# Weight loads and splits placed among the first two batches' chunks of scores in an attention-then-experts kernel

## The chip, the cores and the metric

One core of a Trainium2 chip runs the whole program. The metric is the device time of one execution in microseconds (us); lower is better. The times of before are a median of three runs, and one further execution was profiled. On this core TensorE multiplies matrices, VectorE and ScalarE work elementwise, GpSimd (POOL) issues the indirect stores, and SyncE (SP) issues all other transfers, in order.

## The reference

Four batches of 5056 tokens go through an attention over the 256 channels; each resulting row goes to one of eight experts (the one of the largest logit).

```python
qn = q / (np.linalg.norm(q, axis=1, keepdims=True) + 1e-06)
kn = k / (np.linalg.norm(k, axis=1, keepdims=True) + 1e-06)
s = kn.transpose(0, 2, 1) @ qn / tau        # [B, 256, 256]
a = softmax(s)
x = (v @ a).reshape(B * N, 256)
logits = x @ w_gate                          # [B*N, 8]
e = argmax(logits); gate = softmax(logits)[e]
out = gate * (np.maximum(x @ w1[e], 0) @ w2[e])   # w1 256x1024, w2 1024x256
```

## The kernel before, in words

**Attention of a batch** (`attention`, L182 to L394) is a generator. It first goes through 20 *chunks* of 256 tokens: loads of q and k (L194, L195, 256 KB each), squares on ScalarE (L203) that VectorE adds up to the channel norms (two adds, L207 and L208), and the scores. In a *native* chunk these are four fp32 matmuls (L214, eight pieces in the trace); in a *split* chunk ScalarE and VectorE first write q and k as two parts (L177, L178), which eight faster matmuls use (L218, L219). Batch 0 is native throughout, batch 1 native in chunks 1 to 13. Then come the norms (L227 to L246) and the softmax (L248 to L302), and ten *groups* of 512 tokens: a load of v (L312), v @ a and the gate's logits (`px`, L326 for batch 0, L329 for others), copies and squares on ScalarE (L331, L333), rows as two fp16 parts (L343, L344), the expert and place of each token, and four indirect stores by POOL into the sorted array `xs` (L392).

**Weights** (`weights`, L93 to L162) is a generator over 16 matrices (w1 and w2 of each expert). Each is loaded as two halves of 512 KB (L118, L120) into the place in `W` that the next matrix's parts will fill, so no load waits for a buffer. TensorE forms its Gram matrix from 16 pieces (L134), VectorE takes the diagonal (L137) for the scale of the expert, and each half is later *split* into two fp16 parts: ScalarE writes the high part (L105), VectorE the low one (L106), each 1024 elements per partition.

**Experts** (`block`, L538 to L600) work on *blocks* of 256 sorted rows of one expert: 48 matmuls with w1 (L561), relu and split (L568, L569), 48 with w2 (L584). `table` (L447) makes the list of a stage's blocks from the counts so far; stage 0 is made from batch 0's first six groups (`CUT`).

**The order.** A scheduler emits each engine's queue, in order, close to the order of the code. The opening (L648 to L653) takes all 20 chunks of batch 0, then 14 steps of the weights, then per step one of batch 0 (softmax and half groups), two of the weights and one chunk of batch 1: ten chunks in all. The weight loads are put behind the last q and k load (`last_load`). Then come the first table, batch 0's last four groups, and the blocks. During the blocks the remaining attention runs as side work, in amounts set by planned costs (a chunk 1280 units, a group 2920): `START` (L669) counts what was done ahead, and the first ten blocks share out the rest of batch 1, (START + 59800) / 10 = 4700 units a block.

**Buffers that matter here.** q, k and v share the three `raw` tiles (batch 0's chunks also use `rows` and `xg`); the diagonal and ScalarE's junk squares share one tile, `junk`; the blocks' copies of weight pieces have five tiles, `wp` (L548).

Of the kernel before, what the change touches and what calls it, by code (L numbers as in the profile page):

```python
# [20 lines left out]
P = 128  # L21
# [40 lines left out]
def attention_then_experts(ctx, tc, q, k, vT, tau, w_gate, w1, w2, kc, out):  # L62
# [27 lines left out]
    last_load = [None]  # L90

    def weights():
# [8 lines left out]
        def split_one():  # L101
            nonlocal ready
            if ready:
                hi, lo, src, sw = ready.pop(0)
                act.activation(hi, src, AF.Copy, scale=sw)  # L105
                vec.scalar_tensor_tensor(out=lo, in0=src, scalar=sw, in1=hi, op0=ALU.mult, op1=ALU.subtract)  # L106

        for n in range(2 * E):
            e, w = divmod(n, 2)
            if n < 2 * E - 1:  # L110
                raw = place(n + 1).bitcast(F32)
            else:
                raw = work.tile([P, 2048], F32, tag="hl", name="wraw", bufs=2)
            raw = raw.rearrange("p (h x) -> p h x", h=2)
            for h in range(2):
                with tc.issue_after(last_load[0]):
                    if w == 0:
                        sync.dma_start(out=raw[:, h, :], in_=w1[e, h * P : (h + 1) * P, :])  # L118
                    else:
                        sync.dma_start(  # L120
                            out=raw[:, h, :].rearrange("p (f d) -> p f d", d=C),
                            in_=w2[e, h * 512 : (h + 1) * 512, :].rearrange("(f p) d -> p f d", p=P),
                        )
                split_one()
# [7 lines left out]
            for i in range(16):  # L132
                part = top[:, i * P : (i + 1) * P]
                pe.matmul(own, part, part, start=(i == 0), stop=(i == 15))  # L134
            diag = work.tile([P, P], F32, tag="junk", name="w_diag", bufs=1)
# [8 lines left out]
            for h in range(2):  # L144
                if w == 0:
                    d5 = place(n).rearrange("p (q d s f) -> p q d s f", q=4, d=2, s=2)
                    hi, lo = d5[:, :, h, 0, :], d5[:, :, h, 1, :]
                    src = raw[:, h, :].rearrange("p (q f) -> p q f", q=4)
                else:
                    d4 = place(n).rearrange("p (f s d) -> p f s d", f=8, s=2)  # L150
                    hi, lo = d4[:, 4 * h : 4 * h + 4, 0, :], d4[:, 4 * h : 4 * h + 4, 1, :]
                    src = raw[:, h, :].rearrange("p (f d) -> p f d", f=4)
                later.append((hi, lo, src, sw))
            if w == 1:
                ready, later = ready + later, []
# [25 lines left out]
    def attention(b, s_split, x_split, acc):  # L181
# [5 lines left out]
        ssq = one.tile([P, 512], F32, tag="a_l", name="ssq")  # L187
        nch = len(s_split)
        for ch in range(nch):

            tag, bufs = (("raw", RAW), ("rows", 3), ("xg", 2), ("raw", RAW), ("rows", 3))[ch % 5 if b == 0 else 0]
            raw = work.tile([P, 2, 512], F32, tag=tag, name="raw", bufs=bufs)
            sl = slice(2 * ch, 2 * ch + 2)
            sync.dma_start(out=raw[:, :, 0:C], in_=qv[b][:, sl, :])  # L194
            load = sync.dma_start(out=raw[:, :, C:512], in_=kv[b][:, sl, :])  # L195
            if b == 0:
                last_load[0] = load.ins
# [5 lines left out]
            act.activation(sq, raw, AF.Square)  # L203
            if ch == 0:
# [18 lines left out]


        tp = ps_t.tile([P, 512], F32, tag="tp", name="ntp")
        for i in range(4):
            pe.matmul(tp[:, i : i + 1], ssq[:, i * P : (i + 1) * P], ones[:, 0:1], start=True, stop=True)  # L227
# [20 lines left out]
        soft = work.tile([P, 8, C], F32, tag="hl", name="soft", bufs=2)  # L248
        for c in range(2):
            dg = soft[:, 0, c * P : (c + 1) * P]  # L250
# [9 lines left out]
        if any(s_split):  # L260
            sums = [soft[:, 1 + c, :] for c in range(2)]
# [476 lines left out]
```

## Time and profile before

| | us |
|---|---|
| median of 3 runs | 1236.44 (1236.13 to 1242.23) |
| profiled execution | 1234.98 |
| its span in the profile | 1233.1 |
| batch 0's scores end on TensorE | 41.9 |
| first x matmul | 61.7 |
| first matmul of a block | 159.4 |

The profile names each instruction by its line of the kernel, with its operands (out <- in), and says for an idle engine what released it. Busy times of an engine are unions of its instructions' spans, so waiting inside the queue is what is left. TensorE's granted clock is given per stretch, 1.00 being 2.4 GHz.

### The profile page before, as it was taken

To read this page: it belongs to the slowest core of one execution; us is meant where nothing else is said; L and a number is where in the kernel's file an instruction comes from. 1 tells how busy PE (TensorE), PEld (TensorE's weight loads), DVE (VectorE), ACT (ScalarE), POOL (GpSimd) and SP (SyncE) were. 2 spreads that over 40 slices of the span, in tenths; PEclk is the share of its full clock that TensorE was granted. 3 is DMA by queue.
4 is the path that set the end of the run, shared out by engine and by line. 5 is a ranking of instruction groups with operands and counts; after the bars stand their busy time and mean duration, and the time that the engine had idled before them with its cause. 6 is when DMAs were issued, how large, how long until landed. Compare 5 with 4: busy or idle time off the path is not lost.

```text
span 1233.1 us, 28379 instructions
## 1 busy us (share of the span) xinstructions
PE 1163.7 (94%) x10182; PEld 1027.0 (83%) x10182; DVE 921.1 (75%) x2586; ACT 648.0 (53%) x1378; POOL 356.8 (29%) x326
## 2 busy tenths in 40 slices
PE   8778789988899999999999999999999999999998
PEld 7666577878788888988888888889888888888887
DVE  6787888867798878777788878767676666666886
ACT  5477864666655545656655545666533333332332
POOL 0022451244431112544432111455331111111111
PEclk9879999999999999999999999999999999999999
DMA  9968685434354533344254453342232222211121
GB/s 308 379 226 270 177 199 141 117 104 129 104 149 125 137 95 96 112 128 114 79 143 125 126 111 87 108 113 82 71 106 53 53 53 53 49 48 42 39 49 33
DMA packets 190688, 145.93 MB, mean 118 GB/s; under 512 B 117580, under 2 KB 168145, under 8 KB 190544
## 3 DMA queue, kind: packets, MB, share of 16 engines
q1 hardware_dynamic: 175152, 102.48, 32.7%
q0 software_dynamic: 15392, 41.60, 9.6%
q8 instruction: 81, 1.33, 0.5%
q14 instruction: 63, 0.52, 0.1%
HBM read 80.03 MB, written 43.29 MB: 100 GB/s over the span
## 4 chain that ended last, share of the span: by engine, by line
PE 47%; issue 26%; DVE 6%; POOL 5%; ACT 1%; DMA 1%; POOLq 0%; another core or an unknown queue 0%; DVEq 0%; SPq 0%; ACTq 0%
PE hp L561 17%; PE y L584 17%; PE px L329 6%; POOL out L595 4%; PE sp L218 3%; PE sp L219 2%; DVE ht L569 1%; POOL xs L392 1%; DVE hl L178 1%; DVE rows L344 1%; DVE wp L549 1%; DMA xs<-rows,r_si 1%; ACT ht L568 0%; ACT rows L343 0%; DMA out<-o,mt 0%
## 5 line engine op out<-in xcount | busy, mean ns | idle before, releaser
L584 PE MATMUL y<-wp,ht 128*128 128x256 f16 x3888 | 450.5, 273 | 8.3 <-DVE ht L569 4.6
L561 PE MATMUL hp<-xT,wp 128*128 128x256 f16 (+1 forms) x4320 | 450.1, 262 | 5.8 <-issue 2.5
L584 PEld LDWEIGHTS <-ht 128*128 128x128 f16 x3888 | 373.2, 98 | 68.1 <-issue 11.1
L561 PEld LDWEIGHTS <-wp 128*128 128x128 f16 x4320 | 382.2, 98 | 53.9 <-issue 11.0
L549 DVE COPY wp<-W 128x1024 f16 x720 | 298.6, 428 | 104.1 <-PE y L584 68.5
L595 POOL DMA_INDIRECT out<-o,mt x162 | 182.2, 1125 | 664.0 <-ACT o L593 631.2
L568 ACT ACTIVATE ht<-hp 128x512 f16<-128x512 f32 x324 | 191.5, 595 | 197.2 <-PE hp L561 143.0
L569 DVE SCALAR_TENSOR_TENSOR ht<-hp,ht 128x512 f16<-128x512 f32 x324 | 221.7, 687 | 42.1 <-ACT ht L568 36.7
L392 POOL DMA_INDIRECT xs<-rows,r_si x160 | 174.4, 1090 | 207.9 <-DVE scales L83 82.4
L593 ACT ACTIVATE o<-y,b_fac 128x256 f32<-128x256 f32 x162 | 68.8, 469 | 176.6 <-PE y L584 164.2
L329 PE MATMUL px<-a_h,hl 128*128 128x264 f32 x480 | 100.4, 297 | 6.0 <-ACT xg L331 4.0
L343 ACT ACTIVATE rows<-xg,x_sc 128x256 f16<-128x256 f32 x160 | 69.1, 497 | 34.9 <-DVE x_sc L83 31.1
L329 PEld LDWEIGHTS px<-a_h,hl 128*128 128x128 f32 x480 | 79.7, 190 | 8.3 <-ACT xg L331 5.1
L177 ACT CAST hl<-raw 128x1024 fp32r<-128x1024 f32 x47 | 49.1, 1045 | 49.4 <-PE sp L219 40.1
L214 PE MATMUL sp<-raw 128*128 128x256 f32 x264 | 64.6, 403 | 10.8 <-DMA raw<-in_k 10.8
L178 DVE TENSOR_TENSOR hl<-raw,hl 128x1024 fp32r<-128x1024 f32 x47 | 57.4, 1222 | 22.9 <-ACT hl L177 22.9
L218 PE MATMUL sp<-hl 128*128 128x512 f32 x188 | 73.3, 422 | 0.0
L331 ACT COPY xg<-px 128x264 f32<-128x264 f32 x160 | 58.1, 367 | 26.2 <-PE px L329 7.0
L203 ACT ACTIVATE raw<-raw 128x1024 f32<-128x1024 f32 x47 | 49.7, 1058 | 41.2 <-DVE hl L178 39.4
L329 PE MATMUL px<-a_l,hl 128*128 128x264 f32 x240 | 68.9, 287 | 0.0
L344 DVE SCALAR_TENSOR_TENSOR rows<-xg,x_sc,rows 128x256 f16<-128x256 f32 x160 | 68.7, 477 | 0.2
L333 ACT ACTIVATE xjunk<-xg 128x256 bf16<-128x256 f32 x160 | 66.5, 416 | 3.0
(138 smaller groups left out, 942.9 us busy)
## 6 DMA issues: line engine op xcount, KB each, us to landing
raw<-in_q SPq DMA_DIRECT2D x80, 256.0 KB
raw<-in_k SPq DMA_DIRECT2D x80, 256.0 KB
vraw<-in_vT SPq DMA_DIRECT2D x40, 512.0 KB
W<-in_w SPq DMA_DIRECT2D x30, 512.0 KB
out<-o,mt POOLq DMA_INDIRECT x162
xs<-rows,r_si POOLq DMA_INDIRECT x160
xT<-xs SPq DMA_TRANSPOSE x90
xs<-pad SPq DMA_DIRECT2D x9, 129.0 KB
```

The costliest lines, as they stand in the source:

```text
L178: vec.tensor_tensor(out=hl[:, 1], in0=raw, in1=hl[:, 0], op=ALU.subtract)
L218: pe.matmul(sp[c], hl[:, 0, j, kc0 : kc0 + P], hl[:, :, j, 0:C], start=first, stop=False)
L329: pe.matmul(px, hl[:, vh, c, ts], ah[:, c, :], start=(n == 0), stop=(n == 5))
L343: act.activation(r16[:, t, 0:C], x, AF.Copy, scale=sc[:, t : t + 1])
L344: vec.scalar_tensor_tensor(out=r16[:, t, C : 2 * C], in0=x, scalar=sc[:, t : t + 1], in1=r16[:, t, 0:C], op0=ALU.mult, op1=ALU.subtract,)
L392: ins = pool.indirect_dma_start(out=xs[:, :], out_offset=bass.IndirectOffsetOnAxis(ap=si[:n, t : t + 1], axis=0), in_=rows[:n, t, :], in_o ...
L549: vec.tensor_copy(out=t, in_=Wf[:, ds(e * 8192 + n * 1024, 1024)])
L561: pe.matmul(hp[:, f % nf, :], wp[:, dc, wh, (f % 2) * P : (f % 2 + 1) * P], xT[:, 2 * xh + dc, :], start=(n == 0), stop=(n == 5),)
L568: act.activation(ht[:, 0], hp, AF.Relu)
L569: vec.scalar_tensor_tensor(out=ht[:, 1], in0=hp, scalar=0.0, in1=ht[:, 0], op0=ALU.max, op1=ALU.subtract)
L584: pe.matmul(ys[j], hts[f // nf][:, hh, f % nf, j * P : (j + 1) * P], wp[:, f % 2, wh, :], start=(f == 0 and n == 0), stop=(f == 7 and n == 2),
L595: pool.indirect_dma_start(out=out[:, :], out_offset=bass.IndirectOffsetOnAxis(ap=mt.bitcast(I32)[:, j, 1:2], axis=0), in_=o, in_offset=Non ...
```

## The change

- **Loads.** All of the opening's loads are issued in one written order (`load`). From chunk 2 of batch 0 on, one weight load follows each chunk's q and k; the rest follow two to a step among v and batch 1's chunks.
- **Steps.** Batch 0's chunks 2 to 19 each come with one step of the weights (nine matrices loaded by then, most of their Grams and some splits done). 15 further steps take two of the weights, batch 0's softmax and six groups, and 13 chunks of batch 1 (`OPENING`) instead of 10. `START` follows: 4316 units a block.
- **Splits** take a whole matrix, 2048 elements per partition, in one instruction each on ScalarE and VectorE; only the last matrix is split in four quarters, from `ht` tiles.
- **Buffers.** Batch 0's chunks use three `raw` and three `rows` tiles, its v (groups 0 to 5) the blocks' `wp` tiles with loads up to two groups ahead, its softmax the blocks' `xT` and `o` tiles, its sum of squares an `xg` tile. The diagonal has a tile of its own.
- **Norms of batch 0**: one add of 1024 elements per chunk instead of two of 512, and eight small matmuls instead of four at the end.

```diff
+    def load(out, in_):
+        if opening[0] is None:
+            ins = sync.dma_start(out=out, in_=in_)
+        else:
+            with tc.issue_after(opening[0]):
+                ins = sync.dma_start(out=out, in_=in_)
+        opening[0] = ins.ins
...
-            diag = work.tile([P, P], F32, tag="junk", name="w_diag", bufs=1)
+            diag = work.tile([P, P], F32, tag="diag", name="w_diag", bufs=1)
...
-                later.append((hi, lo, src, sw))
+            d4 = place(n).rearrange("p (k s x) -> p k s x", k=8, s=2)
+            if n < 2 * E - 1:
+                src = place(n + 1).bitcast(F32).rearrange("p (k x) -> p k x", k=8)
+                later.append((d4[:, :, 0, :], d4[:, :, 1, :], src, sw))
+            else:
+                for i in range(4):
+                    ks = slice(2 * i, 2 * i + 2)
+                    later.append((d4[:, ks, 0, :], d4[:, ks, 1, :], raw[i].rearrange("p (k x) -> p k x", k=2), sw))
...
-            tag, bufs = (("raw", RAW), ("rows", 3), ("xg", 2), ("raw", RAW), ("rows", 3))[ch % 5 if b == 0 else 0]
-            raw = work.tile([P, 2, 512], F32, tag=tag, name="raw", bufs=bufs)
+            tag = "rows" if b == 0 and ch % 2 else "raw"
+            raw = work.tile([P, 2, 512], F32, tag=tag, name="raw", bufs=3)
...
+            if b == 0:
+                if ch > 0:
+                    vec.tensor_tensor(out=ssq, in0=ssq, in1=sq, op=ALU.add)
...
+        def v_load(g):
+
+            if g < CUT:
+                raw = [work.tile([P, 512], F32, tag="wp", name="vraw", bufs=WP) for _ in range(2)]
+            else:
+                both = work.tile([P, 2, 512], F32, tag="raw", name="vraw", bufs=RAW)
+                raw = [both[:, 0, :], both[:, 1, :]]
...
+        if b == 0:
+            for g in range(2):
+                v_ahead[g] = v_load(g)
...
+            dgs = work.tile([P, C], F32, tag="o", name="dgs", bufs=2)
+            sums_t, s2, aT = [work.tile([P, 2, C], F32, tag="xT", name=nm, bufs=3) for nm in ("sums", "s2", "aT")]
...
+                raw = v_ahead.pop(g, None) or v_load(g)
+                if g + 2 < G and early():
+                    v_ahead[g + 2] = v_load(g + 2)
...
-    for step in range(2, nch + 1 + 2 * CUT):
+    for ch in range(1, nch):
         take(first, 1)
-        take(wts, 0 if step < nch else 14 if step == nch else 2)
-        if step > nch + 2:
-            take(second, 1)
+        take(wts, 1 if ch > 1 else 0)
+    take(first, 1)
+    for step in range(2 * CUT + 3):
+        if step > 2:
+            take(first, 1)
+        take(wts, 2)
+        take(second, 1 if step < OPENING else 0)
     run(wts)
...
-    START = -(2 * CUT - 2) * 2 * 640
+    START = -OPENING * 2 * 640
```

**How the queues change.** SP's queue where batch 0's loads end, before (`raw` is q and k of a chunk, `W` a half of a weight matrix):

```order
L194 DMA raw_301<-in_q 128x2x256
L195 DMA raw_301<-in_k 128x2x256
L194 DMA raw_312<-in_q 128x2x256
L195 DMA raw_312<-in_k 128x2x256
L118 DMA W_79<-in_w1 128x1024 x2
L120 DMA W_79<-in_w2 128x4x256 x2
L118 DMA W_79<-in_w1 128x1024 x2
L120 DMA W_79<-in_w2 128x4x256 x2
```

and in the changed kernel, some chunks earlier:

```order
L97 DMA raw_210<-in_q 128x2x256
L97 DMA raw_210<-in_k 128x2x256
L97 DMA W_79<-in_w1 128x4x256
L97 DMA raw_223<-in_q 128x2x256
L97 DMA raw_223<-in_k 128x2x256
L97 DMA W_79<-in_w1 128x4x256
L97 DMA raw_254<-in_q 128x2x256
L97 DMA raw_254<-in_k 128x2x256
L97 DMA W_79<-in_w2 128x4x256
```

The weights stood behind the last chunk; now one load of them follows each chunk's pair.

SP's queue where batch 0's v loads begin to wait for buffers, before:

```order
L118 DMA W_79<-in_w1 128x1024 x2
L312 DMA vraw_538<-in_vT 128x2x512
L120 DMA W_79<-in_w2 128x4x256 x2
L118 DMA W_79<-in_w1 128x1024 x2
L312 DMA vraw_665<-in_vT 128x2x512
L120 DMA W_79<-in_w2 128x4x256 x2
L194 DMA raw_722<-in_q 128x2x256
L195 DMA raw_722<-in_k 128x2x256
L118 DMA W_79<-in_w1 128x1024 x2
```

and now, at the load of v for group 2 (two tiles of 256 KB, `vraw_710` and `vraw_711`):

```order
L97 DMA raw_662<-in_q 128x2x256
L97 DMA raw_662<-in_k 128x2x256
L97 DMA W_79<-in_w2 128x4x256 x2
L97 DMA raw_699<-in_q 128x2x256
L97 DMA raw_699<-in_k 128x2x256
L97 DMA vraw_710<-in_vT 128x512
L97 DMA vraw_711<-in_vT 128x512
L97 DMA W_79<-in_w1 128x4x256 x2
L97 DMA raw_764<-in_q 128x2x256
```

Group 2's v stands ahead of the loads of the next weight matrix.

VectorE's queue around batch 0's first group of x, before (`W` with `scales` is a split, `w_diag` a diagonal, `x_sc`, `r_` the group's small steps):

```order
L137 SCALAR_TENSOR_TENSOR w_diag_653,w_dsum_567<-gram_566,kt_104 128x128
L389 TENSOR_REDUCE r_si_631<-r_sl_629 128x4
L82 TENSOR_SCALAR pw_m_656<-gram_566 128x2
L83 TENSOR_SCALAR scales_377<-pw_m_656 128x2
L106 SCALAR_TENSOR_TENSOR W_79<-W_79,scales_377 128x4x256 x2
L352 TENSOR_REDUCE r_m_751<-xg_667 128x4
L354 TENSOR_TENSOR r_d_753<-xg_667,r_m_751 128x32
L357 SCALAR_TENSOR_TENSOR r_eq_755<-r_d_753,kt_104 128x32
L359 TENSOR_REDUCE r_r_757<-r_eq_755 128x4
L106 SCALAR_TENSOR_TENSOR W_79<-W_79,scales_377 128x4x256
L137 SCALAR_TENSOR_TENSOR w_diag_711,w_dsum_694<-gram_693,kt_104 128x128
L106 SCALAR_TENSOR_TENSOR W_79<-W_79,scales_377 128x4x256
```

and now, from the end of the softmax on:

```order
L356 COPY aT_563<-atp_581 128x512
L242 TENSOR_TENSOR ssq_621<-ssq_621,sq_665 128x512
L364 COPY a_x_568<-gtp_587 128x2x8
L113 SCALAR_TENSOR_TENSOR W_79<-W_79,scales_133 128x8x256
L154 SCALAR_TENSOR_TENSOR w_diag_693,w_dsum_643<-gram_642,kt_92 128x128
L241 TENSOR_TENSOR ssq_621<-ssq_621,sq_702 128x512
L82 TENSOR_SCALAR pw_m_696<-gram_642 128x2
L242 TENSOR_TENSOR ssq_621<-ssq_621,sq_702 128x512
L83 TENSOR_SCALAR scales_133<-pw_m_696 128x2
L113 SCALAR_TENSOR_TENSOR W_79<-W_79,scales_133 128x8x256
```

The splits are half as many and twice as long, and chunks of batch 1 (`ssq`) now stand between them from the softmax on.

## Rows read from the trace of the kernel before

**Rows 1.** The page, part 1: busy us, share of the span, instructions.

```profile
PE 1163.7 (94%) x10182; PEld 1027.0 (83%) x10182; DVE 921.1 (75%) x2586; ACT 648.0 (53%) x1378; POOL 356.8 (29%) x326
```

**Rows 2.** Busy time by stage: stretch, its us, each engine, clock, DMA.

```profile
core 0: us, PE busy (x) PEld busy (x) DVE busy (x) ACT busy (x) POOL busy (x), PEclk, DMA share, GB/s
0.00:10.00 10.00, 5.36 (x13) 4.37 (x14) 2.73 (x9) 3.51 (x4) 0.20 (x4) 1.00 0.76 227
10.00:30.00 20.00, 20.00 (x94) 17.60 (x93) 16.84 (x25) 13.77 (x14) 0.00 (x0) 1.00 1.08 346
30.00:60.00 30.00, 23.81 (x180) 21.45 (x178) 22.20 (x60) 12.76 (x16) 0.00 (x0) 0.89 1.07 379
42.70:61.70 19.00, 11.60 (x119) 10.66 (x117) 15.79 (x50) 9.36 (x12) 0.00 (x0) 0.80 1.06 378
61.70:159.40 97.70, 78.31 (x433) 62.10 (x434) 79.53 (x289) 78.35 (x192) 35.47 (x30) 0.90 0.73 222
159.40:320.00 160.60, 145.50 (x1206) 127.89 (x1207) 123.88 (x418) 100.16 (x247) 60.00 (x57) 0.99 0.51 136
320.00:1233.00 913.00, 890.19 (x8261) 793.10 (x8258) 674.19 (x1785) 437.85 (x909) 261.13 (x236) 1.00 0.34 89
```

**Rows 3.** TensorE timeline: start us, us, line, operation, operands, count.

```profile
4.64 37.27 PE L214 MATMUL sp<-raw 128*128 128x256 f32 x160 [4.64 <-DMA raw<-in_k]
...
42.56 1.08 PE L134 MATMUL gram<-W 128*128 128x128 bf16 x16
...
61.66 6.80 PE L326 MATMUL px<-a_x,vraw 128*128 128x264 f32 x16
...
159.40 1.47 PE L561 MATMUL hp<-xT,wp 128*128 128x256 f16 x12
...
167.11 1.89 PE L214 MATMUL sp<-raw 128*128 128x256 f32 x8
```

**Rows 4.** Waits of TensorE, 61.7 to 159.4 us: total us, times, longest.

```profile
PE gram L134 <- DVE w_diag L137: 6.8, 2, 4.2
PE sp L214 <- DMA raw<-in_k: 6.2, 3, 2.3
```

**Rows 5.** Waits of SP (the queue of loads), 61.7 to 159.4 us.

```profile
SPq L194 <- PE sp L214: 11.1, 4, 6.3
SPq L312 <- PE px L326: 10.4, 2, 8.0
```

**Rows 6.** The page, part 6: loads, their count, KB of each.

```profile
raw<-in_k SPq DMA_DIRECT2D x80, 256.0 KB
...
W<-in_w SPq DMA_DIRECT2D x30, 512.0 KB
```

**Rows 7.** VectorE groups, 61.7 to 159.4 us: count, busy us, mean ns, idle before.

```profile
L106 DVE SCALAR_TENSOR_TENSOR W<-W,scales 128x1024 f16<-128x1024 f32 x24 | 30.1, 1281 | 6.2 <-ACT W L105 4.9 <-issue 1.3
L344 DVE SCALAR_TENSOR_TENSOR rows<-xg,x_sc,rows 128x256 f16<-128x256 f32 x32 | 13.7, 478 | 0.0
...
L207 DVE TENSOR_TENSOR ssq<-ssq,sq 128x512 f32<-128x512 f32 x9 | 6.2, 685 | 0.0
...
L137 DVE SCALAR_TENSOR_TENSOR w_diag<-gram,kt 128x128 f32<-128x128 f32 x10 | 2.8, 285 | 2.9 <-PE gram L134 2.9
```

**Rows 8.** Busy time and granted clock of three 10 us stretches (columns of rows 2).

```profile
50.00:60.00 10.00, 7.28 (x62) 6.77 (x61) 7.69 (x20) 5.11 (x9) 0.00 (x0) 0.66 1.06 383
...
80.00:90.00 10.00, 7.43 (x38) 6.39 (x38) 9.80 (x34) 7.53 (x13) 3.36 (x3) 0.66 0.84 280
90.00:100.00 10.00, 7.78 (x48) 6.41 (x47) 7.31 (x17) 8.45 (x19) 4.33 (x4) 1.00 0.93 309
```

**Rows 9.** ScalarE groups, 61.7 to 159.4 us.

```profile
L105 ACT ACTIVATE W<-W,scales 128x1024 f16<-128x1024 f32 x23 | 25.6, 1140 | 6.9 <-DVE scales L83 3.7 <-DVE W L106 3.2
...
L343 ACT ACTIVATE rows<-xg,x_sc 128x256 f16<-128x256 f32 x35 | 14.9, 496 | 2.8 <-DVE x_sc L83 2.6 <-DVE r_r L359 0.2
```

**Rows 10.** TensorE group of native chunks, 61.7 to 159.4 us.

```profile
L214 PE MATMUL sp<-raw 128*128 128x256 f32 x76 | 20.6, 421 | 6.2 <-DMA raw<-in_k 6.2
```

More of the change, by code (lines that the diff above doesn't have):

```diff
@@ L166, in attention_then_experts, with early @@
     WP = 5
+    blocks_begun = [False]
+    def early():
+        return not blocks_begun[0]
     EARLY = 2
+    OPENING = 13
     NATIVE = 14
@@ L186, in attention @@
         sp = [pool_.tile([P, 2, C], F32, tag=tag, name=f"sp{c}") for c, (pool_, tag) in enumerate(acc)]
-        ssq = one.tile([P, 512], F32, tag="a_l", name="ssq")
+        if b == 0:
+            ssq = work.tile([P, 2, 512], F32, tag="xg", name="ssq", bufs=2)
+        else:
+            ssq = one.tile([P, 512], F32, tag="a_l", name="ssq")
         nch = len(s_split)
         for ch in range(nch):
-            tag, bufs = (("raw", RAW), ("rows", 3), ("xg", 2), ("raw", RAW), ("rows", 3))[ch % 5 if b == 0 else 0]
-            raw = work.tile([P, 2, 512], F32, tag=tag, name="raw", bufs=bufs)
+            tag = "rows" if b == 0 and ch % 2 else "raw"
+            raw = work.tile([P, 2, 512], F32, tag=tag, name="raw", bufs=3)
             sl = slice(2 * ch, 2 * ch + 2)
[L194 to L197, printed above, removed]
+            for part, src in ((raw[:, :, 0:C], qv[b]), (raw[:, :, C:512], kv[b])):
+                if early():
+                    load(part, src[:, sl, :])
+                else:
+                    sync.dma_start(out=part, in_=src[:, sl, :])
             if s_split[ch]:
@@ L222, in attention @@
             yield 2 * 640
+        v_ahead = {}
+        def v_load(g):
+            if g < CUT:
+                raw = [work.tile([P, 512], F32, tag="wp", name="vraw", bufs=WP) for _ in range(2)]
+            else:
+                both = work.tile([P, 2, 512], F32, tag="raw", name="vraw", bufs=RAW)
+                raw = [both[:, 0, :], both[:, 1, :]]
+            for c in range(2):
+                if early():
+                    load(raw[c], vv[b][:, c, g * 512 : (g + 1) * 512])
+                else:
+                    sync.dma_start(out=raw[c], in_=vv[b][:, c, g * 512 : (g + 1) * 512])
+            return raw
+        if b == 0:
+            for g in range(2):
+                v_ahead[g] = v_load(g)
         tp = ps_t.tile([P, 512], F32, tag="tp", name="ntp")
         for i in range(4):
-            pe.matmul(tp[:, i : i + 1], ssq[:, i * P : (i + 1) * P], ones[:, 0:1], start=True, stop=True)
+            cs = slice(i * P, (i + 1) * P)
+            if b == 0:
+                for j in range(2):
+                    pe.matmul(tp[:, i : i + 1], ssq[:, j, cs], ones[:, 0:1], start=(j == 0), stop=(j == 1))
+            else:
+                pe.matmul(tp[:, i : i + 1], ssq[:, cs], ones[:, 0:1], start=True, stop=True)
         def four(name):
@@ L260, in attention @@
         if any(s_split):
-            sums = [soft[:, 1 + c, :] for c in range(2)]
+            sums = [sums_t[:, c, :] for c in range(2)]
             for c in range(2):
@@ L292, in attention @@
                 )
-        aT = soft[:, 5:7, :]
         vec.tensor_copy(out=aT, in_=tp.rearrange("p (c n) -> p c n", c=2))
@@ L617, in attention_then_experts @@
     second = attention(1, [i == 0 or i >= NATIVE for i in range(nch)], True, normal)
-    take(first, 2)
+    take(first, 1)
     kt = one.tile([P, K_TRI], F32, name="kt")
-    sync.dma_start(out=kt, in_=kc[:, 0:K_TRI])
+    load(kt, kc[:, 0:K_TRI])
     ident = kt[:, K_ID : K_ID + P]
@@ L627, in attention_then_experts @@
     tri32 = work.tile([P, P], F32, tag="junk", name="tri32", bufs=1)
-    sync.dma_start(out=tri32, in_=kc[:, K_TRI:K_N])
+    load(tri32, kc[:, K_TRI:K_N])
     vec.tensor_copy(out=tri, in_=tri32)
```

80 lines of the change are left out of this document (45 added, 35 removed).

## The prediction, made before the changed kernel had run

> **What bounds the kernel now.** I began with the busy shares of the page: TensorE is busy 94% of the span, VectorE 75% [rows 1]. That average hides two parts, so I cut the span by stage [rows 2]. From 320 us to the end TensorE is busy 890 of 913 us and from 159.4 to 320 us 145.5 of 160.6: there only less matmul work, or less of the 15 us idle before 320, can save time. From 42.7 to 159.4 us it is busy 11.6 of 19.0 and 78.3 of 97.7 us, part of it at the lower clock (mean granted clock 0.80 and 0.90). The change works in this opening. I call the stretches A (batch 0's chunks of scores, to 41.9 us), B (first softmax, to 61.7), C (x groups, the second batch's first chunks and the weights, to the first block at 159.4) and D (the rest). Their ends are in TensorE's timeline [rows 3].
>
> What paces each? In A TensorE works without a gap: 160 pieces (8 a chunk) from 4.64 us for 37.3 us, 1.86 us per chunk [rows 3]. Batch 0's loads meanwhile run at 346 GB/s, and the weights, behind them, at 379 GB/s [rows 2]. In C no engine is full: VectorE has 79.5, ScalarE 78.4 and TensorE 78.3 us busy of 97.7 [rows 2], so about a fifth of C is waiting on one another. The waits that TensorE shows there are for q and k (6.2 us) and for the diagonals of weight Grams on VectorE (6.8 us) [rows 4]. And SP, which issues every load in one line, stood 10.4 us on x matmuls before v loads and 11.1 us on scores matmuls before q loads [rows 5].
>
> **The change, part by part, against the profiled execution (1234.98 us).**
>
> *A: weight loads among batch 0's chunks.* A's last k load now has 20 chunks at 2 x 256 KB (10.5 MB) and 17 weight loads of 512 KB (8.9 MB) before or with it [rows 6]. The first 10 us moved 2.27 MB (227 GB/s). The remaining 8.2 MB of q and k at 346 GB/s take 23.7 us, the 8.9 MB of weights at 379 GB/s 23.5 us [rows 2]: the last k lands at 57.2 us, and its chunk ends at 59.1 us on TensorE. Before it was 41.9 us: A costs 17.2 us more. Cover: per chunk the loads take 2.9 us. TensorE has 1.86 us of scores and half of a Gram (1.08 us for 16 pieces [rows 3]), about 2.5 us with the small ones. VectorE has one add (below 2 x 0.69 us [rows 7]) and up to half of a whole-half split (2.35 us, below), also some 2.6. So loads set A, narrowly; VectorE is the next in line.
>
> A now feeds TensorE in bursts with a short wait for a load after each. Where that happened before, the record is mixed: at 78% busy the granted clock was 1.00 (90 to 100 us), at 73 to 74% it was 0.66 (50 to 60 and 80 to 90 us) [rows 8]. A's 2.5 of 2.9 us is 86%, so I take full clock. The Trainium skill (TensorE: Matmul & The Clock Gate, HAM oscillation — how this bites in real kernels) speaks against this change: it tells of a loop whose matmuls wait for a transfer after each burst and start each burst at the lower clock. By that rule the time would be that of the last rival below, 1249 us; no row here has bursts with waits as short as A's 0.4 us, and the 78% row above does not follow the rule.
>
> *B: the first softmax in other buffers.* The chain itself is unchanged: 41.9 to 61.7 us, 19.8 us. In VectorE's queue it had the other six of the 32 half-size splits between its steps (26 lie in C [rows 7]) and now has three whole ones, one subtraction and some adds. I take B as equal: first x matmul at 78.9 us. Grams, and batch 1's first two chunks, fill TensorE there at no cost.
>
> *C: what is no longer in it.* VectorE: 26 half-size splits go (24 in 30.1 us [rows 7] and the last matrix's two at the same price, 32.6); six whole-size and four quarter-size ones come. No whole one stands in the trace; 256 elements took 478 ns and 1024 took 1281 [rows 7], 1.05 ns per further element, which gives 2.35 us for 2048 and 0.75 for 512. Two halves end to end, 2.56 us, is the upper bound; twice the step alone, 2.14, the lower. I take 2.35: 17.1 us. Five diagonals fewer (285 ns each) and one pair of adds more (1.4 us) cancel. So VectorE has 15.5 us less: 64 us. ScalarE: 25 halves of 1.14 us go (23, and the last matrix's two); by the same slope (496 ns at 256 elements, 1140 at 1024 [rows 9]) five whole ones cost 2.0 us each and four quarters 0.71: 15 us less, 63 us. TensorE: 96 Gram pieces fewer (0.067 us each, 6.5 us); the split first chunk lies in B now (3.4 us, not quite two native ones); 1.5 more native chunks (2.8 us): 7.1 us less, 71 us.
>
> If the waits stayed, C would shrink by VectorE's 15.5 us to 82.2. Some must go: v of batch 0 now has the blocks' weight buffers, so chunks and v no longer queue for the same three, and the diagonal no longer shares the buffer in which ScalarE drops its squares. These two stood behind 13 us of TensorE's waits [rows 4]. A new one comes: on SP the second half of the v load for group 2 waits for group 0's x matmuls, and the next weight loads stand behind it, whose Gram TensorE has right behind those matmuls. From nothing to 4 us (a load's transfer and landing), at two places, partly under VectorE's backlog. I take 5 us net off: C = 77 us, first block at **156 us** instead of 159.4. Bounds: C is not below VectorE's 64 us (block at 143), and not above TensorE's 71 us at the old utilisation, 0.80, 89 us (block at 168).
>
> *D.* At the first block 13 chunks of batch 1 are done; before 10.5 (the split one, and 76 native pieces of 8 a chunk [rows 10]). The 2.5 chunks come out of a stretch that TensorE bounds, at 1.89 us each [rows 3]: 4.7 us. The blocks' side work in the first ten blocks falls from 4700 to 4316 planned units per block; 8% of the 15 us idle before 320 is 1.2 us. Past that nothing moves.
>
> Sum: 3.4 (block earlier) + 4.7 + 1.2 = 9.3 us; 1234.98 - 9.3 = 1225.7. The median of the runs shown is 1.5 us above the profiled execution, so I predict **1227 us**.
>
> **Rivals.**
> 1. *The opening interleaves well.* All of C's waits for loads and diagonals go, and VectorE is nearly full: C = 66 us, block at 145, 14.4 + 5.9 = 20.3 us gained, 1216 us. For: the waits of [rows 4] name what is removed. Against: three engines with 63 to 71 us each in 66 us leave no room, and their queues are in order.
> 2. *The time only moves.* A's 17.2 us is paid in full and C keeps its utilisation because SP again waits, now for the x groups, with the weights behind it: C = 86 us, block at 165, 5.5 us lost against 5.9 gained in D: 1236 us. For: C's three engines all stood at 80% before, with the waits spread out. Against: the loads that SP held up are mostly done by then.
> 3. *Slower: TensorE falls to the lower clock in A.* The place is between the chunks, where it now waits for loads. 2.48 us per chunk at full clock is 4.13 at a mean clock of 0.60, against 2.9 us for the loads: 18 chunks x 1.23 = 22 us, block at 178, 1227 + 22 = 1249 us. It costs from a mean clock of 0.86 down, and cancels the gain at about 0.73 (3.4 us per chunk). For: 0.66 in [rows 8]. Against: the clock stayed at 1.00 at 78% busy, and an engine that slows down is busier.
>
> **How the numbers follow.** A measurement of this kernel can tell about 0.5% from no change, 6.2 us: below 1230.3 is faster, above 1242.6 slower. The forecast has 0.5 (1221 to 1233; 0.42 faster, 0.08 same), rival 1 0.2 (faster), rival 2 0.2 (0.04 faster, 0.15 same, 0.01 slower), rival 3 0.1 (0.01 same, 0.09 slower). Together 0.66 faster, 0.24 same, 0.10 slower. The range runs from 1214 (C at its lower bound of 64 us, 22.3 us gained) to 1239 (C at its upper bound of 89 us, 2.6 us lost); it leaves out rival 3 and the tails.
>
> **What would show it.** Right: batch 0's scores on TensorE end at 57 to 61 us with the DMA at 340 GB/s or more all through and the clock at 1.00; first x matmul at 77 to 81 us; VectorE at 64 to 68 us busy in C; first block at 150 to 162 us with 13 chunks done; after it the same profile as before, some 6 us shorter. Wrong: a clock below 0.86 in A; A ending before 54 us (loads faster than any row); SP idle for over 5 us on an x matmul between 80 and 100 us with TensorE's Gram waiting for the load behind it; or a stretch past 320 us that differs by more than 2 us.

## The result and the profile after

The changed kernel takes 1251.4 us (median of 4, 1246.96 to 1252.02) beside 1236.3 us for the kernel before (median of 4): a ratio of 1.0108, 95% interval 1.0073 to 1.0142. The forecast was 1227 us, with a range from 1214 to 1239. The profiled execution took 1252.02 us (span 1250.3).

The stretches A to D in the changed kernel, in the columns of [rows 2] (us, busy us of each engine, granted clock, DMA share, GB/s):

```profile
0.00:64.90 64.90, 49.24 (x301) 39.76 (x302) 40.76 (x56) 35.68 (x28) 0.20 (x4) 1.00 1.04 329
64.90:87.80 22.90, 14.89 (x113) 12.68 (x110) 17.03 (x44) 10.77 (x11) 0.00 (x0) 0.70 0.66 210
87.80:175.80 88.00, 71.25 (x336) 55.43 (x337) 67.23 (x259) 64.19 (x173) 30.74 (x28) 0.90 0.67 203
175.80:1250.30 1074.50, 1037.00 (x9446) 919.43 (x9445) 796.55 (x2196) 536.29 (x1155) 319.23 (x294) 0.99 0.36 95
```

| us | before | forecast | after |
|---|---|---|---|
| A, to the end of batch 0's scores | 41.9 | 59.1 | 64.9 |
| B, to the first x matmul | 19.8 | 19.8 | 22.9 |
| C, to the first block | 97.7 | 77 | 88.0 |
| D, the rest | 1073.7 | 5.9 less | 1074.5 |

A, B, C and D missed by 5.8, 3.1, 11 and 6.7 us. TensorE's timeline at the boundaries and at the largest waits of B and C (columns of [rows 3]; in brackets the idle time before, and who ended it):

```profile
63.00 1.94 PE L248 MATMUL sp<-raw 128*128 128x256 f32 x8
...
67.28 1.95 PE L283 MATMUL ntp<-ones,ssq 128*128 128x1 f32 x16 [1.54 <-DVE ssq L237]
...
74.71 1.22 PE L316 MATMUL ntp<-dgs,ones 128*128 128x128 f32 x4 [3.69 <-DVE dgs L315]
...
78.56 0.79 PE L252 MATMUL sp<-hl 128*128 128x512 f32 x1 [2.17 <-DVE hl L202]
...
87.82 1.16 PE L393 MATMUL px<-a_x,vraw 128*128 128x264 f32 x4
...
97.55 0.40 PE L151 MATMUL gram<-W 128*128 128x128 bf16 x2 [3.95 <-DMA W<-in_w]
...
114.00 0.19 PE L442 MATMUL rtp<-r_oh,tri 128*128 128x32 f16 x1 [3.34 <-DVE r_oh L428]
115.05 0.40 PE L151 MATMUL gram<-W 128*128 128x128 bf16 x2 [0.87 <-DMA W<-in_w]
...
165.43 0.21 PE L442 MATMUL rtp<-r_oh,tri 128*128 128x32 f16 x1 [4.62 <-remote]
...
175.82 1.47 PE L628 MATMUL hp<-xT,wp 128*128 128x256 f16 x12
```

The 3.95 us before 97.55 are a wait for a weight load. Why that load was late stands in SP's timeline. A row there is an issue (or several, x2), and the second number says how long SP was on it:

```profile
73.23 0.71 SPq L97 DMA_DIRECT2D raw<-in_k  x1
73.99 19.54 SPq L97 DMA_DIRECT2D vraw<-in_vT  x2
93.57 1.22 SPq L97 DMA_DIRECT2D W<-in_w  x2
...
99.84 10.74 SPq L97 DMA_DIRECT2D vraw<-in_vT  x2
110.64 1.31 SPq L97 DMA_DIRECT2D W<-in_w  x2
...
118.43 9.17 SPq L97 DMA_DIRECT2D vraw<-in_vT  x2
```

The second half of v for group 2 needs a `wp` tile that group 0's x matmuls free. These come behind the softmax, so SP stood from 74 to 93.5 us with weight loads ready behind it. What that did, in windows of 10 us:

```profile
50.00:60.00 10.00, 8.33 (x59) 6.64 (x57) 8.12 (x8) 6.38 (x6) 0.00 (x0) 1.00 1.10 348
...
70.00:80.00 10.00, 4.14 (x20) 3.41 (x21) 8.26 (x25) 3.49 (x5) 0.00 (x0) 0.50 0.94 301
80.00:90.00 10.00, 9.65 (x65) 8.26 (x65) 7.81 (x14) 6.16 (x10) 0.00 (x0) 0.83 0.01 2
90.00:100.00 10.00, 6.05 (x26) 4.22 (x24) 7.15 (x21) 7.58 (x15) 0.00 (x0) 0.85 0.53 168
...
110.00:120.00 10.00, 5.73 (x27) 3.79 (x27) 7.49 (x19) 7.11 (x16) 3.39 (x2) 0.71 0.85 270
```

From 80 to 90 us the DMA moved 2 GB/s. From 90 to 100 us TensorE then lacks its weight load and is busy 6.05 us of 10. From 110 to 120 us it is busy 5.73 us: it waits 3.34 us for a routing step of VectorE and right behind it 0.87 us for the weight load that SP issued at 110.64. Its granted clock is 0.85 and 0.71 in these two windows. The 4.62 us at 165.43 come much later, and the profile names no engine of this core for them.

### The profile page after: what moved, and what is told of

Its sections match the earlier page's. It is cut to its first block, busy times and chain, and to the rows that moved or that the text cites. A ratio compares the mean times of both kernels' runs of the same rounds, so it can differ in the third digit from the quotient of the medians.

```text
span 1250.3 us, 28315 instructions
## 1 busy us (share of the span) xinstructions
PE 1172.4 (94%) x10190; PEld 1027.3 (82%) x10190; DVE 921.6 (74%) x2553; ACT 646.9 (52%) x1365; POOL 350.2 (28%) x326
## 4 chain that ended last, share of the span: by engine, by line
PE 52%; issue 27%; POOL 6%; DMA 5%; DVE 5%; ACT 2%; SPq 1%; another core or an unknown queue 0%; POOLq 0%; DVEq 0%; ACTq 0%
PE hp L628 19%; PE y L651 17%; PE px L396 7%; POOL out L662 4%; DMA raw<-in_k 4%; PE sp L252 3%; PE px L393 2%; POOL xs L459 2%; PE sp L253 2%; PE sp L248 1%; DVE hl L202 1%; DMA W<-in_w 1%; ACT W L112 1%; DVE ht L636 1%; SPq L97 1%
## 5 line engine op out<-in xcount | busy, mean ns | idle before, releaser
L459 POOL DMA_INDIRECT xs<-rows,r_si x160 | 168.8, 1055 | 218.0 <-DVE rows L447 115.9
L248 PE MATMUL sp<-raw 128*128 128x256 f32 x264 | 68.5, 405 | 16.5 <-DMA raw<-in_k 16.4
L248 PEld LDWEIGHTS sp<-raw 128*128 128x128 f32 x264 | 50.2, 201 | 28.0 <-DMA raw<-in_q 10.7
```

Source lines behind the costliest of these rows:

```text
L248: pe.matmul(sp[c][:, 0, :], raw[:, j, kc0 : kc0 + P], raw[:, j, 0:C], start=first, stop=last)
L459: ins = pool.indirect_dma_start(out=xs[:, :], out_offset=bass.IndirectOffsetOnAxis(ap=si[:n, t : t + 1], axis=0), in_=rows[:n, t, :], in_o ...
```

## The experiments

Each ratio is against the kernel before on the same chip, since chips differ: the kernel before takes 1206 to 1209 us on three of them, and 1236 to 1243 in the first result and on the chip of experiment 6. The changed kernel itself ran on these slower ones alone, so what an edit to it gains elsewhere is a difference of ratios from two chips. "Block" is the first block's start in that kernel's profile.

**1. Does the blocked queue cost the time?** The v loads one group ahead, so two more steps of weights stand before the waiting one:

```diff
-                if g + 2 < G and early():
-                    v_ahead[g + 2] = v_load(g + 2)
+                if 1 <= g < G - 1 and early():
+                    v_ahead[g + 1] = v_load(g + 1)
```

> Edit: in the opening, v for group g+1 (from the second group on) is loaded at the start of group g, where the changed kernel loads v for g+2; so two more steps of weight loads and q and k loads stand on SP ahead of the v load that waits for group 0's x matmuls. Theory 1 (SP blocked): in the changed kernel SP stood 19.5 us on that v load (74.0 to 93.5 us) while the DMA queues ran empty, and the Gram behind it held TensorE 3.95 us and left it at a granted clock of 0.71 to 0.85 until 120 us. Then the DMA moves over 200 GB/s from 80 to 90 us (2 before), TensorE's waits for weight loads between 90 and 120 us go, the first block starts at 164 to 171 us instead of 175.8, and the time is 1240 to 1247 us. Theory 2 (the loads held up were not needed earlier; VectorE's and ScalarE's queues set the pace): first block at 174 to 177 us, time 1250 to 1252 us. Theory 3 (the block only moves on, to the q and k loads that wait for a buffer): SP still idles over 8 us between 75 and 95 us, block 171 to 175 us.

Ratio 0.9989 (0.9974 to 1.0004), block at 163.0 in the profiled execution, which was the slowest of the twelve (1214.0 us, median 1207.4): the whole loss is gone. SP and stretch C:

```profile
75.50 1.22 SPq L97 DMA_DIRECT2D W<-in_w  x2
85.62 0.37 SPq L97 DMA_DIRECT2D raw<-in_q  x1
...
88.89 7.03 SPq L97 DMA_DIRECT2D vraw<-in_vT  x2
```

```profile
90.20:163.00 72.80, 64.22 (x336) 50.66 (x337) 64.25 (x262) 62.91 (x174) 35.59 (x30) 1.00 0.75 224
```

Theory 1, with one sign missed: from 80 to 90 us the DMA moved 142 GB/s, not over 200. C is 72.8 us at full clock, and was 88.0 at 0.90. TensorE has no wait for a weight load in it. SP still stands some 9 us before the q load at 85.62 (theory 3 in part), with little left behind it that is urgent.

**2. Is it the queue, or the order of the loads?** The changed kernel with v of groups 2 on issued by GpSimd, at the same places, into the same buffers:

```diff
-                if early():
+                if early() and g >= 2:
+                    pool.dma_start(out=raw[c], in_=vv[b][:, c, g * 512 : (g + 1) * 512])
+                elif early():
```

> Edit: of the changed kernel only this: v of the groups from 2 on, while no block has begun, is loaded by GpSimd's queue instead of SP's, at the same places and with the same buffers; the wait for the x matmuls is now in a queue that has no weight loads behind it. Theory 1 (what cost the time was that the weight loads stood behind that wait on SP): as e1_v_later, first block at 160 to 168 us, SP's waits on x matmuls before L97 gone, DMA over 150 GB/s from 80 to 90 us, ratio to the kernel before 0.996 to 1.002. Theory 2 (e1_v_later gained because v itself, or the q and k beside it, came in another order, not because of the queue): ratio 1.008 to 1.013, as the changed kernel. Theory 3 (GpSimd's queue delays the scatters behind its own waits): first block after 170 us with SP free.

Ratio 1.0029 (1.0014 to 1.0043), a little past the band, and the block where theory 1 has it, at 164.4:

```profile
89.40:164.40 75.00, 66.69 (x335) 52.98 (x336) 64.06 (x258) 63.84 (x177) 42.33 (x41) 0.95 0.68 208
```

From 80 to 90 us the DMA moves 192 GB/s. The v loads still wait for the x matmuls, on GpSimd now:

```profile
95.03 1.11 POOL L269 DMA_DIRECT2D vraw<-in_vT  x2 [93.02 <-PE px L395]
```

Only what stood behind them changed. So it is the queue.

**3. The rate of the loads.** w1 as whole rows, the split reading its source in the order that results:

```diff
-                            own.rearrange("p (q d f) -> p q d f", q=4, d=2)[:, :, h, :],
-                            w1[e, h * P : (h + 1) * P, :].rearrange("p (q f) -> p q f", q=4),
+                            own[:, h * 1024 : (h + 1) * 1024],
+                            w1[e, h * P : (h + 1) * P, :],
```

> Edit: the halves of w1 are loaded as whole rows of 4 KB into place, as in the kernel before, and the split's source is read in another order (two splits of half the size, back to back, for a w1 matrix); the changed kernel loads w1 in pieces of 1 KB. Theory 1 (the size of the pieces sets the rate, 348 GB/s in the changed kernel's first stage against 379 for the weights before): the weights go at about 379 GB/s again, 8.9 MB in 23.5 us instead of 25.6, the scores of batch 0 end at 62 to 63.5 us instead of 64.9, the first block comes 1.5 to 3 us earlier, time 1248.5 to 1250.5 us. Theory 2 (the mixture with q and k, whose pieces are 1 KB, holds the rate at 348 whatever w1 does): scores end at 64.5 to 65.5 us, DMA 345 to 350 GB/s, time 1251 to 1252.5 us (the six more half-size splits cost VectorE 0.2 us each).

Ratio 1.008 (1.0064 to 1.0096). The scores end at 63.3 us, and the rate is the same in every window:

```profile
20.00:30.00 10.00, 8.93 (x57) 7.04 (x55) 7.60 (x12) 7.35 (x7) 0.00 (x0) 1.00 1.08 364
...
50.00:60.00 10.00, 8.02 (x54) 6.60 (x53) 8.64 (x14) 6.46 (x7) 0.00 (x0) 1.00 1.08 364
```

Theory 1 for the stage: 364 GB/s where the changed kernel had 348. The scores end 1.6 us earlier, the block does not come earlier (176.5): SP stood 19.7 us behind group 0 all the same.

**4. Splits at half size**, two per matrix:

```diff
-                later.append((d4[:, :, 0, :], d4[:, :, 1, :], src, sw))
+                for i in range(2):
+                    ks = slice(4 * i, 4 * i + 4)
+                    later.append((d4[:, ks, 0, :], d4[:, ks, 1, :], src[:, ks, :], sw))
```

> Edit: the splits at half size again, two per matrix at the two places of its steps, all else as changed. Theory 1 (a whole split of 2.35 us in VectorE's queue stands inside the chain of the first softmax and ahead of subtractions that TensorE waits for): the stretch from the end of batch 0's scores to the first x matmul shrinks from 22.9 to 20 to 21.5 us and the first block comes 1 to 3 us earlier; time 1248 to 1250.5 us, although VectorE has 0.2 us more per matrix. Theory 2 (size does not matter; only the sum on VectorE does): 15 more splits with 0.2 us of overhead each, first block 0 to 3 us later, time 1251 to 1254.5 us.

Ratio 1.009 (1.0075 to 1.0104), B 22.7 us. The softmax chain is no shorter, against theory 1. In the profiled execution, its slowest (1229.6 us, median 1220.1), the block came at 182.5, with A at a mean clock of 0.97. The ratio is a little below what either theory meant, and its interval overlaps the changed kernel's: the size of the splits is at most a small part of the loss.

**5. Without the mixing**, the 18 steps in a bunch behind the softmax, first alone:

```diff
-        take(wts, 1 if ch > 1 else 0)
     take(first, 1)
+    take(wts, 18)
```

> Edit: no weights among batch 0's chunks; the same 18 steps of weights are taken together behind the first softmax, all else as changed (buffers, whole splits, 13 chunks ahead, v loads). Theory 1 (mixing costs more than it gives, because the first stage is bound by loads while the softmax behind it waits for all of batch 0): scores of batch 0 end at 41 to 43 us, first x matmul at 61 to 66, and the first block, with the same Grams and splits behind it, at 156 to 168 us; time 1232 to 1243 us. Theory 2 (the mixing itself is paid back and the loss comes from the blocked SP queue): the first block stays at 172 to 178 us, because SP still blocks on v with weights behind it and the 18 steps come late; time 1248 to 1255 us.

Ratio 1.0067 (1.0052 to 1.0082), between the theories; the block, at 173.5, is where theory 2 has it. The scores end at 41.9 us, the first x matmul comes only at 78.2 behind nine matrices' Grams, and SP stands 15.9 us on the v load. With the later v loads too:

> Edit: the later v loads of e1_v_later and no weights among batch 0's chunks (as in e3_no_mix) together. With SP no longer held, what is the mixing itself worth? Theory 1 (mixing pays once SP runs on, because Grams and splits are done beside the loads): without it the time is 6 to 12 us above e1_v_later, ratio to the kernel before 1.004 to 1.009, about that of e3_no_mix. Theory 2 (mixing costs, whatever SP does; the 17 to 23 us that the end of batch 0's scores moves are never won back): ratio 0.990 to 0.997.

Ratio 1.0007 (0.9995 to 1.0019), block at 161.0. Neither theory: against a bunch of 18 steps the mixing gives some 0.2% (0.9989 in experiment 1, on another chip), and the intervals overlap.

**6. The changed kernel and the kernel before again, and 10 chunks ahead** (`OPENING = 10`), on one chip, for stretch D:

> No edit: the changed kernel again, beside the others on one chip, because the chip of the first four experiments runs the kernel before in 1208.7 us where the first took 1236.3. Theory 1 (what separates the chips is the stretch of blocks alone, 1041 against 1074 us): ratio to the kernel before 1.008 to 1.012, batch 0's scores end at 64 to 68 us and the first block at 174 to 180 us, as in the changed kernel's first profile. Theory 2 (the loss hangs on the chip): ratio 0.99 to 1.005.

> No edit: the kernel before, for its profile on the same chip. First block at 158 to 161 us as in its first profile. Theory 1 (the 2.5 chunks that the changed kernel has done ahead are worth nothing in the stretch of blocks): the stretch from the first block to the end is within 2 us of the changed kernel's on this chip. Theory 2 (they are worth the predicted 4.7 to 5.9 us, and lower clock and idle in the first blocks hid that on the first chip): it is 4 to 7 us longer than the changed kernel's.

> Edit: 10 chunks of the second batch ahead of the first block instead of 13; all else as changed. Theory 1 (the chunks are worth in the stretch of blocks what they cost in the opening): the first block 4 to 6 us earlier, the stretch behind it 4 to 6 us longer, the time within 2 us of the changed kernel's, ratio to the kernel before 1.007 to 1.012. Theory 2 (the stretch of blocks takes the same whatever was done ahead, so the chunks cost their place in the opening in full): ratio 1.002 to 1.006. Theory 3 (three chunks more among the blocks are split ones' neighbours and cost VectorE there): ratio over 1.013.

Ratios 1.0119 (1.0092 to 1.0146), 1.0 (0.9978 to 1.0023) and 1.011 (1.008 to 1.0139); blocks at 178.1, 160.4 and 174.0. D's first 200 us and its rest, of the kernel before, of the changed one, and with 10 chunks:

```profile
160.40:360.40 200.00, 180.15 (x1486) 157.44 (x1487) 157.43 (x526) 124.52 (x298) 83.26 (x73) 0.98 0.50 131
360.40:1240.00 879.60, 858.07 (x7981) 763.27 (x7979) 641.05 (x1678) 414.02 (x860) 237.01 (x220) 1.00 0.34 88
```

```profile
178.10:378.10 200.00, 176.61 (x1453) 153.52 (x1453) 153.00 (x517) 120.14 (x294) 79.64 (x74) 0.97 0.43 122
378.10:1259.30 881.20, 861.98 (x7995) 765.50 (x7993) 642.60 (x1680) 415.07 (x862) 238.29 (x221) 1.00 0.34 88
```

```profile
174.00:374.00 200.00, 180.13 (x1461) 156.93 (x1460) 154.34 (x520) 122.08 (x293) 83.98 (x72) 0.97 0.47 129
374.00:1256.40 882.40, 863.25 (x8012) 767.33 (x8009) 644.87 (x1685) 417.52 (x865) 242.02 (x222) 1.00 0.34 88
```

Three chunks more ahead leave TensorE 3.5 us less busy in the first 200 us (180.13 to 176.61) and shorten D by 1.2 us (1082.4 to 1081.2). So c_before's theory 1 stands (D is 1079.6 us there): what was done ahead became idle time. Between c_before and c_after a lower clock in the first 200 us (0.98 and 0.97) has a part too, for over all of D TensorE is busy 1038.2 and 1038.6 us, with 2.5 chunks less in the second. e5's ratio is in the band of its theory 1, but its block is 4.1 us earlier and D only 1.2 us longer.

**7. The diagonal's own buffer alone**, in the kernel before; then that kernel again as c_diag, on another chip:

```diff
-            diag = work.tile([P, P], F32, tag="junk", name="w_diag", bufs=1)
+            diag = work.tile([P, P], F32, tag="diag", name="w_diag", bufs=1)
```

> Edit: the kernel before with one part of the change alone: the diagonal of a Gram in a buffer of its own, not in the one in which ScalarE drops its squares. Theory 1 (that sharing stood behind TensorE's 6.8 us of waits for diagonals, as the prediction took it): TensorE's waits for diagonals between the first x matmul and the first block fall below 4 us and the first block comes 1 to 4 us earlier, ratio 0.997 to 0.9995. Theory 2 (the diagonals wait for VectorE's backlog, not for the buffer): waits stay at 5 to 8 us, ratio 0.9995 to 1.0015.

> No edit beside e10_before_diag (the kernel before with a buffer of its own for the diagonal): the reference of this call. If its gain belongs to the kernel and not to one chip, ratio 0.992 to 0.997 again; if it was chance, 0.998 to 1.002.

Ratios 0.9941 (0.9921 to 0.9962) and 0.9972 (0.9958 to 0.9985): this one line beats both kernels. Theory 1, and more: the block comes at 153.5 and 153.6, some 6 to 7 us earlier than in the two profiles of the kernel before (159.4 and 160.4). TensorE's waits for diagonals in C, first of c_before, then of e10_before_diag (us in total, times, longest):

```profile
PE gram L134 <- DVE w_diag L137: 7.3, 2, 4.2
```

```profile
PE gram L141 <- DVE w_diag L137: 0.9, 2, 0.4
PE gram L134 <- DVE w_diag L137: 0.8, 2, 0.4
```

Taken out of the changed kernel it is worth little:

> Edit: the changed kernel without its one part that gained: the diagonal again in the buffer in which ScalarE drops its squares. Theory 1 (the buffer is worth its 7 us in either order): TensorE's waits for diagonals come back with 5 to 8 us between the first x matmul and the first block, ratio to the kernel before 1.015 to 1.020. Theory 2 (in the changed order two thirds of the Grams are done before ScalarE drops squares, so the buffer is worth little): ratio 1.010 to 1.014.

Ratio 1.0132 (1.0116 to 1.0148), whose interval overlaps c_after's, and no such wait among TensorE's in C: theory 2.

**8. One part more beside the diagonal.** v in the `wp` tiles, no look-ahead:

> Edit: to the kernel before with the diagonal's buffer comes one more part of the change, v of batch 0's first six groups in the buffers of the blocks' weights, so that it no longer shares three buffers with q and k; no mixing, no look-ahead. Theory 1 (SP's 21.5 us of waits on x matmuls before v loads stood behind idle time, as the prediction took it): those waits fall below 12 us, the first block comes 1 to 4 us earlier than c_diag's, ratio to the kernel before 0.990 to 0.994. Theory 2 (VectorE and ScalarE pace that stretch, and v's places cost or give nothing): ratio within 0.0015 of c_diag's. Theory 3 (the wait only passes to another load behind it): SP's sum of waits between 62 and 150 us stays within 5 us of c_diag's.

Ratio 0.9971 (0.9958 to 0.9983), as c_diag: theory 2, though the block comes 3.5 us later (157.1). Theory 3's sign is there as well: SP's 22.3 us on x matmuls before v fell to 3.3, one of 13.8 us of a q load on VectorE's rows came, and the sum of SP's waits from 62 to 150 us hardly moves, 64.9 and 68.7 us. And the mixing alone:

```diff
-        take(wts, 0 if step < nch else 14 if step == nch else 2)
+        take(wts, 1 if step < nch else 0 if step == nch else 2)
```

> Edit: to the kernel before with the diagonal's buffer comes the mixing alone: one step of weights after each of batch 0's chunks from the third on, none in a bunch behind the softmax; splits at half size, v and buffers as in the kernel before. Theory 1 (the mixing itself is what costs beside the blocked queue, since batch 0's scores end about 18 us later and the softmax, x groups and routing behind them are a chain that must follow): the first block 3 to 12 us later than c_diag's, ratio to the kernel before 0.998 to 1.005. Theory 2 (the mixing pays for itself, the Grams and splits being out of the way later): ratio 0.988 to 0.996.

Ratio 1.0053 (1.0037 to 1.0069), just past theory 1's band, beside 0.9972 for c_diag: theory 1. The first three stretches of c_diag and of e12_diag_mix:

```profile
0.00:42.30 42.30, 37.02 (x162) 31.63 (x163) 27.57 (x46) 22.44 (x21) 0.20 (x4) 1.00 1.00 325
42.30:61.40 19.10, 11.34 (x128) 10.51 (x126) 15.79 (x50) 9.36 (x12) 0.00 (x0) 0.86 1.06 379
61.40:153.60 92.20, 76.16 (x436) 60.56 (x437) 78.36 (x285) 79.23 (x192) 35.75 (x29) 0.94 0.78 237
```

```profile
0.00:62.10 62.10, 49.81 (x296) 40.15 (x296) 44.78 (x82) 36.45 (x36) 0.20 (x4) 1.00 1.02 343
62.10:79.70 17.60, 6.09 (x25) 5.25 (x25) 10.97 (x33) 4.09 (x7) 0.00 (x0) 0.56 0.92 322
79.70:159.50 79.80, 68.22 (x394) 54.30 (x395) 66.28 (x270) 68.36 (x179) 32.05 (x28) 0.97 0.69 195
```

Mixing puts the first x matmul 18.3 us later and gets 12.4 us back in C, so the block is 5.9 us later. B then holds almost nothing but the softmax: TensorE is busy 6.09 of 17.6 us, at half clock most of the time (0.56).

**9. The repairs together**: later v loads, w1 in rows, then with 10 chunks ahead as well.

> Edit: the later v loads of e1_v_later and the 4 KB rows of w1 of e2_w1_rows together. Theory 1 (the two act at different places and add): batch 0's scores end at 63 to 65 us, the first block 1 to 3 us before that of e1_v_later (163.0, and some 160 in its faster runs), at 157 to 161 us, ratio to the kernel before 0.996 to 0.9985. Theory 2 (once SP runs on, the last weight load paces the opening no longer and an earlier end of the scores is lost in waits of x groups): ratio 0.998 to 1.001, as e1_v_later alone.

> Edit: later v loads, 4 KB rows of w1, and 10 chunks of the second batch ahead instead of 13. Theory 1 (three chunks ahead cost the opening 4 us and the stretch of blocks gives 1 back, as e5_opening10 showed beside c_after): ratio to the kernel before 0.995 to 0.998, the fastest so far. Theory 2 (with SP running on the chunks fill time that is idle otherwise): ratio 0.998 to 1.001.

Ratios 0.9989 (0.9967 to 1.0011) and 0.9983 (0.997 to 0.9995), blocks at 166.8 and 158.4. e6 ran on the chip of c_after, 1241.7 us beside 1258.6: the loss goes there too. The rows of w1 add nothing to experiment 1 that can be measured (theory 2), and the block comes later, not earlier. e8's ratio is just inside the band of its theory 2, its interval reaches into that of theory 1, and the two are not told apart; it is 0.2% faster than the kernel before, and stays behind the one line of experiment 7 (0.9941 on the same chip).

## Why the prediction was wrong, step by step

**The step that failed most** is in C: "From nothing to 4 us (a load's transfer and landing), at two places". The wait was named, with its place and what is queued behind it, but priced as one load's delay. It is a head-of-line stop: SP can go on only when group 0's x matmuls have run, and those are a whole softmax away. It lasted 19.5 us, then 10.7 and 9.2. Without it C is 72.8 us (experiment 1) or 75.0 (experiment 2), where 77 was forecast, and the block comes at 163.0 or 164.4. In e6 it comes at 166.8 with C at 82.8, which begins some 6 us earlier there. So C's other terms, VectorE's 15.5 us and the 5 us of waits, were about right together, and this one wait is what lost most of C's 11 us. Of the 15.2 us between the changed kernel's C and experiment 1's, the lower clock took 7.0 (TensorE is busy 71.25 and 64.22 us on the same 336 matmuls) and idle time 8.2. That all of these 8.2 us come from SP's stop is not shown: the 4.62 us at 165.43 are among them.

At the level of the time, the ratio goes from 1.0108 and 1.0119 to 0.9989 without the stop, which is still no gain: the forecast was 0.992, and the misses in A, B and D are the rest. Rival 2 had the mechanism, with C = 86 us, at a chance of 0.2; against it stood "the loads that SP held up are mostly done by then". They were not. The prediction's own sign, SP idle for over 5 us on an x matmul with the Gram's load behind it, came true.

**A, 59.1 forecast, 64.9.** One step is "the 8.9 MB of weights at 379 GB/s". That rate belonged to a mixture with w1 in whole rows; the change loads w1 in pieces of 1 KB, and everything came at 348. (19.4 - 2.1) MB at 348 GB/s after the first 10 us puts the last k at about 59.7, not 57.2. But at that time only the last chunk but one had its k, as ScalarE's squares of it show:

```profile
59.82 1.06 ACT L234 ACTIVATE sq<-raw 128x1024 f32<-128x1024 f32 x1 [1.94 <-DMA raw<-in_k]
```

One chunk's q and k and a weight load, 1.05 MB, take 3.0 us at 348 GB/s, so the last k came at about 62.7 (an estimate), and its chunk ran at 63.00. So loads set A to its end, as forecast. By then some 1 MB more had moved than the sum counts: loads that SP had issued behind the last k ran beside it, a second step that was left out. In experiment 3 the rate is 364 GB/s, and A ends at 63.3.

**Rival 3, the clock in A**, did not happen in this profile: 1.00 in all of A, with TensorE busy 6.8 to 8.5 of each 10 us from 10 to 60 us. The Trainium skill (TensorE: Matmul & The Clock Gate, HAM oscillation — how this bites in real kernels) tells of bursts that wait for a transfer for longer than they work, and then start at the lower clock. A's waits for q and k were shorter than its bursts (up to 1.24 us, some 6.7 us in 11 waits), and this trace does not show it. It is not ruled out for good, since two profiles have A at 0.95 and 0.97 (experiments 1 and 4). In experiment 1 the clock fell to 0.50 right behind two short waits, and TensorE's next chunk took 3.64 us instead of 1.97:

```profile
32.37 0.63 PE L151 MATMUL gram<-W 128*128 128x128 bf16 x8 [0.90 <-DMA W<-in_w]
33.96 3.64 PE L248 MATMUL sp<-raw 128*128 128x256 f32 x8 [0.96 <-DMA raw<-in_k]
```

The changed kernel's profile has the same two waits, of 0.98 and 0.96 us, at full clock; what decides between the two is not known from these runs. The clock also fell in B: 0.50 from 70 to 80 us, busy 4.14 us.

**B, "equal", cost 3.1 us more.** The step is "The chain itself is unchanged". The norms' first step on VectorE, in the kernel before and in the changed one, and a split among the steps behind it:

```profile
42.73 0.16 DVE L233 TENSOR_SCALAR n_ss<-ntp 128x4 f32<-128x4 f32 x1 [3.48 <-PE ntp L227]
```

```profile
69.27 0.16 DVE L291 TENSOR_SCALAR n_ss<-ntp 128x4 f32<-128x4 f32 x1 [1.83 <-PE ntp L283]
...
69.98 2.35 DVE L113 SCALAR_TENSOR_TENSOR W<-W,scales 128x2048 f16<-128x2048 f32 x1
```

That first step comes 0.8 us after the scores' end before, and 4.4 us after it now: the last chunk's add stood behind a split on VectorE, and the norms' eight matmuls take 1.95 us where four took 0.95. The split at 69.98 stands between the norms' steps, so TensorE waits 3.69 us for the diagonals; what comes behind them is 2.4 us shorter than before. Halves did not shorten B (experiment 4), so the split's size is not the cause.

**D, 5.9 us less forecast, 0.8 more.** The step "The 2.5 chunks come out of a stretch that TensorE bounds" is wrong: they come out of the first 200 us, where TensorE idles some 20 us, mostly on VectorE and ScalarE, and where work taken away becomes idle time or goes into a lower clock (experiment 6). What paces that stretch is not settled.

**What was right.** Whole splits at 2.35 us (measured 2.35 on VectorE, 2.00 on ScalarE), VectorE's 64 us in C (67.2, and 64.25 in experiment 1), 13 chunks done at the first block, and the same length past D's first 200 us (873.6 us before, 874.5 after).

**The parts of the change.** SP's stop costs 0.9 to 1.3% (experiments 2 and 1 beside c_after, on different chips; with e6, on one chip, 1.3%). The mixing costs 0.8% against the kernel before with its bunch of 14 steps (experiment 8). The diagonal's buffer gives 0.3 to 0.6% there and about nothing in the new order. v's places give nothing by themselves. These do not add up to the measured 1.1%: with the stop gone the changed kernel is 0.6% better than the diagonal and the mixing alone (0.9989 beside 1.0053, on different chips), and which of its other parts gives that was not tried.

## What to carry to other kernels

Price a wait on an issuing queue by when its releaser runs, and by all that is queued behind it until then; a load for a buffer that a later stage frees belongs behind every load that waits for nothing. Work moved ahead counts only if the stretch it leaves has no idle time already. And try the smallest part of a change by itself: here one buffer of 64 KB gave 0.3 to 0.6%, where the whole change lost 1.1%.

## What had not been expected of the hardware

- **The rate of loads follows the size of the pieces above 1 KB too.** 348 GB/s with all pieces 1 KB (A of the changed kernel), and 364 with about a quarter of the bytes in 4 KB rows, by that edit alone (experiment 3). The 378 and 379 in B of [rows 2] and of c_diag, with half of the bytes in such rows, go the same way, though no run changed that alone. The Trainium skill (DMA: Bandwidth & Descriptors, Why small descriptors are slow (HBM only)) tells of a fixed cost of each packet; the direction agrees, and that this cost is all of the difference is not shown.
- **Chips differ in one stretch.** D takes 1074 to 1082 us in the first result and on the chip of experiment 6, and 1041 to 1049 on the three others, with TensorE idle 42.6 us there in c_after and 18.2 us in e9_v_pool. A to C are within a few us in the nearest pair of kernels: the block comes at 178.1 in c_after and at 174.6 in e13_after_junk, on a faster chip, where D is 1045.0 us instead of 1081.2. No one kernel was profiled on both kinds of chip, and why D differs is open.
